# Weight transfers of a recurrent-attention loop issued by SyncE and ScalarE in turn

## The chip, the cores and the metric

The kernel runs on one core of a Trainium2 chip. The metric is device time in microseconds (us). Engines are named as in the profile: PE (TensorE, matmuls), PEld (its weight loads), DVE (VectorE), ACT (ScalarE), POOL (GpSimd), SP (SyncE, which here does nothing but issue transfers). SPq, ACTq and POOLq are the engines' sequencers when they issue DMAs. 16 DMA engines move the data.

## The reference, cut to what matters

Two independent heads, joined along the last axis. Head A is a shifted product and a long convolution over 2048 positions (in the kernel, a transform by matmuls). Head B is a recurrence over 64 segments of 32 rows; the eight memory rows of a segment are the first rows of the output of the one before:

```python
for s in range(n_seg):                      # 64
    h = concatenate([mem, x[:, 32*s:32*s+32]], axis=1)      # 8 + 32 rows, 1024 wide
    q, k, v = (einsum('btd,dhe->bhte', h, W) for W in (Wq, Wk, Wv))   # 32 heads of 128
    p = softmax(where(mask, einsum('bhqe,bhke->bhqk', q, k) * scale, -1e9))
    o = einsum('bhte,hed->btd', einsum('bhqk,bhke->bhqe', p, v), Wo)
    mem = o[:, :8]; outs.append(o[:, 8:])
```

Each segment needs all of Wq, Wk, Wv and Wo, 32 MB in bf16, and no segment can begin before the one before has ended.

## The kernel before, in words

The first 440 us hold head A and everything of head B that doesn't depend on the memory (the projections of the last 8 rows of each segment, written to QKBd and VBd). The rest is the loop of L913: 64 segments, one after another, and it is here that the change lies.

A segment has four groups g of 8 heads. For each group `qk_part` (L740) multiplies by 8 pairs of weight tiles (Wq and Wk, one pair for each 128 rows of the model width), `qk_out` (L752) copies the sums to `qks`, `v_part` (L756) multiplies by 4 pairs of Wv, `tr_a` (L779) transposes q and k, `v_out` (L769) copies v. `scores` (L800), `softmax` (L822) and `pv` (L838) of group g run inside the matmuls of the groups after it; `pv` ends in four copies OT (L853). Then `wo` (L857) multiplies by 4 pairs of Wo for each group into `yacc`. At the turn of the segment ACT copies yacc to Y_sb (L957), PE transposes it (`mt_tp`, L895), DVE puts it into hT (L896), and the next segment's matmuls start from hT. In every fourth segment `wo` also works for 4 x 8 set-aside rows (OTB).

The weights come in 64 pairs of 512 KB. Most of them stay on chip. Two pairs are parked in PSUM and copied into place by ACT and DVE (`unpark`, L711). The other 17, `STREAM` (L42), are read again from DRAM in each segment: qk 2 and 5 of group 0, 3 of group 1, 2 and 6 of groups 2 and 3; v 0 and 3 of group 0, 1 of group 1, 2 of groups 2 and 3; o pair 2 of group 0 (here o0_2), o1_1, o2_0, o2_3 and o3_2. They go through a ring of RING = 4 tiles named `wring` that the parked pairs use too. `place` (L703) takes the next key of the list `todo` (17 x 64 keys in order of use), takes the next ring tile, and issues its transfer; `done` (L720) calls it after the last matmul that reads a pair. So a transfer waits until PE has used the pair that the slot held four places before: o3_2 is put into the slot of o0_2, the next segment's first pair into that of o1_1, and so on.

The kernel is scheduled by hand: each engine does its instructions in the order in which the program writes them. A transfer stands in its issuing engine's queue where `place` is called, and what that engine has behind it waits until it is issued. In the loop SP issues the ring's transfers (L708) and four small loads per segment, qkb (L792). ACT issues one load per segment, H (L657). POOL issues the loads of VB (L797) and the stores (L968, L973).

Of the kernel before, what the change touches and what calls it, by code (L numbers as in the profile page):

```python
# [21 lines left out]
def fused_kernel(ctx: ExitStack, tc, q, k, v, shift_k, ssm_k, ssm_D, outa, x, mem0, Wq, Wk, Wv, Wo, outb, n_seg):  # L22
# [11 lines left out]
    nc = tc.nc  # L34
# [26 lines left out]
    Wst = {key: dram.tile([128, 2, 1024], BF, name=f"Wst{key[0]}{key[1]}_{key[2]}") for key in streamed}  # L61
# [639 lines left out]
    todo = [key for _ in range(n_seg) for key in streamed]  # L701

    def place():  # L703

        if todo:
            key = todo.pop(0)
            t = ring.tile([128, 2, 1024], BF, tag="wring", name="wring")
            nc.sync.dma_start(t[:], Wst[key][:])  # L708
            placed.setdefault(key, []).append(t)

    def unpark():  # L711
# [8 lines left out]
    def done(key):  # L720
        if key in res:
            return
        if key in PARKED:
            t = ring.tile([128, 2, 1024], BF, tag="wring", name="wring")
            placed[PARKED[key]] = [t]
            to_copy.append((PARKED[key], t))
        else:
            place()
# [174 lines left out]
    for _ in range(RING):  # L903
        place()
# [139 lines left out]
```

## Time and profile before

| what | us |
|---|---|
| median of 3 runs | 2319.94 (2311.4 to 2321.02) |
| the profiled execution | 2336.46 |
| its span, first to last instruction | 2334.6 |
| from the first Y_sb (L957) to the last, 63 segments | 1859.8 |
| ring transfers: number, size, median time from issue to landing | 1088, 512 KB, 5.3 to 5.6 |

A page of the profile has the engines' busy time, the span in 40 slices, the DMA queues, the chain of work that ended last (followed back from the last instruction), the costliest groups of instructions and the DMA issues. Further views answer questions on the same execution: the waits (who stood idle for whom), a timeline, and the busy time in stretches that one names. In the lists of queues, q1 is SP's hardware queue, q10 is ACT's, q0 is POOL's.

### The profile page before, as it was taken

The numbers are of one execution on the slowest core, as the hardware profiler recorded it, in microseconds if no ns is written. First come the engines' busy times: TensorE is split into PE (matmuls) and PEld (weight loads), VectorE is DVE, ScalarE is ACT, GpSimd is POOL, SyncE is SP. The second block draws the span as 40 slices with busy tenths as digits, with TensorE's granted clock in tenths as the row PEclk, the third lists the DMA queues.
The fourth block names the chain that finished last, engine by engine and source line by source line (L and its number), as shares of the span: only waits on it lengthen the run. The fifth ranks groups of instructions, "written<-read, shape, count | busy, mean of one in ns | idle before, by whom it ended". The sixth has DMA issues, their size and how long they took to land.

```text
span 2334.6 us, 90400 instructions
## 1 busy us (share of the span) xinstructions
PE 1830.9 (78%) x38867; PEld 1056.3 (45%) x38896; DVE 1023.9 (44%) x3490; ACT 827.8 (35%) x2294; POOL 586.3 (25%) x1177
## 2 busy tenths in 40 slices
PE   5779887588787778787877887888787878888875
PEld 3332233345444445454545454545454545554543
DVE  6878722244433344444444443343444343434442
ACT  5457611233333333333333333333333333333332
POOL 4005612013131213122213131313131313131312
PEclk8999989799999999999999999999999998999998
DMA  7799796899988999999899998999999998989995
GB/s 267 261 342 364 264 357 260 299 329 325 314 296 304 301 313 315 324 314 326 307 318 314 326 316 307 309 339 310 340 307 316 315 334 295 332 302 322 314 326 184
DMA packets 279035, 724.19 MB, mean 310 GB/s; under 512 B 78171, under 2 KB 91435, under 8 KB 278121
## 3 DMA queue, kind: packets, MB, share of 16 engines
q1 hardware_dynamic: 239246, 677.88, 82.9%
q0 software_dynamic: 30496, 34.31, 4.6%
q8 instruction: 304, 4.98, 0.8%
q10 hardware_dynamic: 8892, 6.23, 0.8%
q14 instruction: 97, 0.79, 0.1%
HBM read 672.01 MB, written 55.05 MB: 311 GB/s over the span
## 4 chain that ended last, share of the span: by engine, by line
DMA 48%; PE 30%; issue 5%; DVE 2%; ACT 2%; POOL 1%; SPq 0%; POOLq 0%; ACTq 0%; DVEq 0%
DMA wring<-Wstv 22%; DMA wring<-Wstqk 13%; DMA wring<-Wsto 10%; PE qkacc L748 10%; PE yacc L869 8%; PE vacc L763 4%; PE otacc L848 2%; PE tp L776 1%; PE otacc L850 1%; DMA QKBd<-stq 1%; ACT Y_sb L957 1%; PE S L804 1%; PE mt_tp L895 1%; ACT OT L853 1%; DMA Wo<-in_B_Wo_dram 0%
## 5 line engine op out<-in xcount | busy, mean ns | idle before, releaser
L748 PE MATMUL qkacc<-Wqk,hT 128*32 128x512 bf16 x6144 | 520.9, 400 | 4.8 <-issue 1.1
L855 POOL COPY OTB<-OT 128x64 bf16<-128x64 bf16 x256 | 61.0, 238 | 1363.8 <-ACT OT L853 1363.8
L853 ACT CAST OT<-otacc 128x80 bf16<-128x80 f32 x1024 | 181.5, 230 | 504.3 <-PE otacc L850 497.3
L763 PEld LDWEIGHTS <-hT 128*32 128x32 bf16 x8192 | 227.4, 98 | 247.8 <-issue 165.3
L748 PEld LDWEIGHTS <-hT 128*32 128x32 bf16 x8192 | 184.6, 98 | 303.8 <-issue 169.5
L748 PE MATMUL qkacc<-wring,hT 128*32 128x512 bf16 x2048 | 214.1, 405 | 106.7 <-DMA wring<-Wstqk 104.7
L869 PEld LDWEIGHTS <-OT 128*32 128x32 bf16 x8192 | 224.6, 98 | 125.9 <-issue 112.5
L869 PE MATMUL yacc<-Wo,OT 128*32 128x256 bf16 x5632 | 270.3, 282 | 8.3 <-issue 8.0
L763 PE MATMUL vacc<-wring,hT 128*32 128x256 bf16 x3072 | 146.2, 281 | 144.4 <-DMA wring<-Wstv 143.0
L763 PE MATMUL vacc<-Wv,hT 128*32 128x256 bf16 x5120 | 227.1, 278 | 0.0
L785 DVE COPY QT<-tp 128x256 bf16<-128x256 bf16 x256 | 74.3, 290 | 310.3 <-PE tp L776 309.7
L818 DVE TENSOR_REDUCE mx<-S 128x4 f32<-128x160 f32 x256 | 83.1, 325 | 283.6 <-PE S L815 283.6
L869 PE MATMUL yacc<-wring,OT 128*32 128x256 bf16 x2560 | 145.6, 282 | 73.3 <-DMA wring<-Wsto 67.2
L771 ACT CAST vsb<-vacc 128x256 bf16<-128x256 f32 x256 | 95.3, 372 | 242.0 <-PE vacc L763 240.5
L754 ACT CAST qks<-qkacc 128x512 bf16<-128x512 f32 x256 | 149.5, 584 | 75.4 <-PE qkacc L748 70.3
L714 ACT COPY wring<-park 128x1024 bf16<-128x1024 bf16 x128 | 129.9, 1015 | 107.2 <-PE qkacc L748 101.4
L848 PE MATMUL otacc<-PT,vsb 32*128 32x64 bf16 x2048 | 149.6, 193 | 22.6 <-ACT OT L853 21.5
L797 POOL DMA_DIRECT2D VB<-VBd x256 | 150.9, 596 | 28.2 <-issue 18.5
L824 ACT ACTIVATE E<-S 128x160 bf16<-128x160 f32 x256 | 77.6, 303 | 213.6 <-PE qkacc L748 114.8
L850 PE MATMUL otacc<-PT,VB 32*128 32x64 bf16 x2048 | 145.7, 189 | 3.7 <-issue 3.7
L888 DVE COPY hT<-x_tp 128x192 bf16<-128x192 bf16 (+1 forms) x64 | 16.5, 258 | 294.9 <-PE x_tp L887 294.9
L973 POOL DMA_DIRECT2D out_dram<-YB x256 | 126.7, 502 | 42.2 <-DMA out_dram<-YB 23.5
(213 smaller groups left out, 2900.8 us busy)
## 6 DMA issues: line engine op xcount, KB each, us to landing
wring<-Wstqk SPq DMA_DIRECT2D x448, 512.0 KB, 5.3
wring<-Wstv SPq DMA_DIRECT2D x320, 512.0 KB, 5.4
wring<-Wsto SPq DMA_DIRECT2D x320, 512.0 KB, 5.6
SK<-s_sb SPq DMA_DIRECT2D x8, 1024.0 KB, 6.8
SU<-s_sb SPq DMA_DIRECT2D x8, 1024.0 KB, 6.4
QKBd<-stq POOLq DMA_DIRECT2D x4, 2048.0 KB, 9.9
Kg<-SK SPq DMA_DIRECT2D x16, 512.0 KB, 7.2
Ug<-SU SPq DMA_DIRECT2D x16, 512.0 KB, 8.1
```

The source lines that it names most:

```text
L714: nc.scalar.copy(t[:, 0, :], park[key][0][:])
L748: nc.tensor.matmul(u.qk[p0:p0 + 32, :], lhsT=hT[:, kc, :], rhs=w[:, t, c2 * 512:(c2 + 1) * 512], start=(kc == 0), stop=(kc == 7), tile_pos ...
L754: nc.scalar.copy(u.qks[:], u.qk[:])
L763: nc.tensor.matmul(u.vacc[32 * c:32 * c + 32, 0:256], lhsT=hT[:, kc, :], rhs=w[:, kc % 2, c * 256:(c + 1) * 256], start=(kc == 0), stop=(k ...
L771: nc.scalar.copy(u.v[:], u.vacc[:, 0:256])
L797: nc.gpsimd.dma_start(VB[32 * c:32 * c + 32, :], VBd[8 * s:8 * s + 8].rearrange("r (g c x) -> c g r x", g=4, c=4)[c])
L818: nc.vector.tensor_reduce(out=mx[:], in_=S[:], op=ALU.max, axis=AX.X)
L848: nc.tensor.matmul(o, lhsT=u.v[r, i * 128:(i + 1) * 128], rhs=PTv[r, i, 0], start=True, stop=False, tile_position=(32 * c, 0))
L850: nc.tensor.matmul(o, lhsT=VB[r, i * 128:(i + 1) * 128], rhs=PTv[r, i, 1], start=False, stop=True, tile_position=(32 * c, 0))
L853: nc.scalar.copy(u.OT[:, 2 * c:2 * c + 2, :], ov[:, :, 0:40])
L869: nc.tensor.matmul(Y[32 * dq:32 * dq + 32, 256 * n:256 * n + 256], lhsT=lhsT, rhs=w[:, hh % 2, dq * 256:(dq + 1) * 256], start=(u.g == 0 a ...
L973: nc.gpsimd.dma_start(outb[r0:r0 + 8, dq * 256:(dq + 1) * 256], YB[32 * dq + 8 * jj:32 * dq + 8 * jj + 8, :])
```

## The change

One line of `place`. The transfer was always issued by SP; now it is issued by SP when the number of keys left is odd, and by ACT when it is even.

```diff
             key = todo.pop(0)
             t = ring.tile([128, 2, 1024], BF, tag="wring", name="wring")
-            nc.sync.dma_start(t[:], Wst[key][:])
+            (nc.sync if len(todo) % 2 else nc.scalar).dma_start(t[:], Wst[key][:])
             placed.setdefault(key, []).append(t)
```

The matmuls, the ring, the keys and their order are the same. In the program that is built, 544 of the 1088 transfers stand in ACT's queue among its copies and activations. As each segment has 17 of them, what SP issues in one segment ACT issues in the next.

## The prediction

> **What bounds the kernel now.** I read the page first (shares, slices, chain), then the waits of PE, then stretches of one segment of the loop (L913), then SyncE's issues, and last the one place where two hardware queues already run together.
>
> ```profile
> PE 1830.9 (78%) x38867; PEld 1056.3 (45%) x38896; DVE 1023.9 (44%) x3490; ACT 827.8 (35%) x2294; POOL 586.3 (25%) x1177
> ...
> q1 hardware_dynamic: 239246, 677.88, 82.9%
> ...
> DMA 48%; PE 30%; issue 5%; DVE 2%; ACT 2%; POOL 1%; SPq 0%; POOLq 0%; ACTq 0%; DVEq 0%
> ```
>
> The chain that ended last is half DMA. ACT is busy a third of the time, so it has room; SyncE's and ACT's issuing is 0% of the chain. The issuing is therefore not the bottleneck.
>
> ```profile
> PE vacc L763 <- DMA wring<-Wstv: 143.0, 187, 3.0
> ...
> PE yacc L869 <- DMA wring<-Wsto: 67.2, 108, 2.7
> PE otacc L848 <- ACT OT L853: 21.5, 63, 0.3
> ```
>
> These are PE's waits inside the loop (total us, times, longest). With 81.9 us on Wstqk, PE stands still 292 us for streamed weights over 64 segments, 4.6 us in each. ACT holds it 0.34 us once per segment.
>
> ```profile
> 1518.00:1526.00 8.00, 5.44 (x130) 3.21 (x122) 2.14 (x9) 1.38 (x6) 3.62 (x8) 0.88 0.96 327
> 1526.00:1528.00 2.00, 2.00 (x32) 0.82 (x28) 0.78 (x2) 0.92 (x1) 1.10 (x3) 0.65 0.79 281
> 1528.00:1530.00 2.00, 2.00 (x52) 1.26 (x48) 0.24 (x2) 1.23 (x4) 0.00 (x0) 1.00 0.64 189
> 1530.00:1546.00 16.00, 14.11 (x392) 8.94 (x384) 9.21 (x38) 6.43 (x23) 0.71 (x3) 1.00 1.00 368
> ```
>
> Columns: stretch, us, busy us of PE, PEld, DVE, ACT, POOL, then PEclk, DMA share, GB/s. The first row is the end of a segment and its turn (the mean segment is 29.5 us, from the starts of Y_sb L957). DMA is full for 16 us, nearly full at the end, and idles only after the turn: then all four ring slots hold data that PE has not reached. So the loop is a closed circle: a slot is consumed, refilled, and lands 5.3 to 5.6 us later (part 6 of the page), and the 16 engines are the bound except at the turn. More bandwidth is to be had only there.
>
> **The turn, where the change bites.**
>
> ```profile
> 1517.85 0.32 SPq L708 DMA_DIRECT2D wring<-Wsto  x1
> 1518.50 1.47 SPq L708 DMA_DIRECT2D wring<-Wstqk  x2
> ...
> 1523.61 0.40 PE L869 MATMUL yacc<-wring,OT 128*32 128x256 bf16 x8 [1.48 <-DMA wring<-Wsto]
> ...
> 1524.37 0.37 ACT L957 CAST Y_sb<-yacc 128x256 bf16<-128x256 f32 x1 [2.53 <-PE yacc L869]
> ```
>
> The last transfer of the segment (o, group 3, pair 2) is issued at 1517.85 and PE waits 1.48 us for it, until 1523.61. Everything behind it hangs on it: yacc, Y_sb, the transpose, hT and the next segment's first matmul. The two transfers issued behind it (1518.50 and 1519.5) are wanted only after the turn: PE reads the first at 1526.38. One queue serves them in order, so they do not disturb it.
>
> **What the change does, part by part.** L708 issues 1088 transfers. By the parity of the remaining list 544 stay on SyncE and 544 go to ACT. Neighbours always go to different queues; 17 per segment is odd, so two segments take opposite halves. Bytes, ring and consumption stay; PE, DVE and POOL keep their order.
>
> *Sharing between the queues* is the largest term. At the start of the kernel L259 loads KS_nat from both queues; the DMA view of 5 to 10 us shows
>
> ```profile
> DMA packets 567, 2.06 MB, mean 413 GB/s; under 512 B 63, under 2 KB 63, under 8 KB 567
> ...
> q1 hardware_dynamic: 283, 1.03, 51.2%
> q10 hardware_dynamic: 284, 1.04, 51.0%
> ```
>
> Packets of the same 4 KB rows pass turn by turn, half each, and the engines are full either way; the loop's full stretch is at share 1.00 from one queue. So two queues give no bandwidth, they only change the order: a transfer at the head of one queue runs at half rate while the other queue has work. At 413 GB/s 524,288 bytes take 1.27 us. If o3_2 starts together with its neighbour on the other queue, it lands 1.27 us later; if they are half a transfer apart, 0.64 us; if the neighbour is late, 0. PE then waits so much longer, and the DMA idles so much longer after the turn. I take 0.64, in the middle: the issues from 1517.85 to 1520.77 come 0.65 to 1.25 us apart, around one service time. 63 turns x 0.64 = 40 us (0 to 80). Inside the full 16 us an older transfer also lands later, but the next one no later than before, and a full DMA loses nothing; I set that at 0, and upwards 20 us (63 x 0.3).
>
> By the Trainium skill (DMA: Bandwidth & Descriptors, section "Queues, rings and completion order") each DMA engine goes round its queue rows packet by packet; 283 against 284 packets agree.
>
> *ACT's time.* A SyncE issue takes 0.32 us (L708 above). ACT's own: KS_nat (the same 4 KB rows) 0.39 to 0.86, median 0.45; H (L657, short rows) 0.55. I take 0.45: 544 x 0.45 = 245 us on an engine that is idle 1507 us. An ACT issue waits for PE to finish the slot's old weights, and all that stands behind it in ACT's order needs a later PE step, so the wait itself holds nothing up. What counts is the issue's length, at two places. (a) Behind o3_2 the refill stands ahead of Y_sb: released at 1524.0 it ends at 1524.5, Y_sb began at 1524.37, so 0.14 us later in the half of segments where this refill is ACT's: 32 x 0.14 = 4.5 us. (b) Behind o2_3 it stands ahead of the four copies L853 that PE waits for: SyncE issued at 1520.77, ACT would end at 1521.22, the copies began at 1521.03: 32 x 0.19 = 6 us. At 0.32 these are 0 and 2, at 0.86 18 and 19. Together 10 (2 to 37). The copies qks and vsb behind other issues have over 1 us of matmuls (v_part) or a whole group in hand; if that cover went, each 0.45 us would come on top (third rival).
>
> *SyncE's time* is a gain. 97 of its L708 issues come 0.04 us behind another issue with no wait of their own, often behind a qkb load (L792, 0.43 us). Half of them move, each at most 0.43 us earlier, 0.2 in the mean: 48 x 0.2 = 10 us, of which PE feels what it was waiting for. I take 5 (0 to 22; the upper end: SyncE issues for 1088 x 0.32 + 256 x 0.43 = 458 us, 24% of the loop's 1880, so a release meets a running issue with that chance and waits half of it, 0.04 us per transfer, 44 us, of which half moves).
>
> The four small queues (VB, stores, H) now share with two big queues instead of one. VB lands 4.8 us after issue and is wanted a third of a segment later, H a group later: nothing.
>
> Sum: 40 + 10 - 5 = +45 us. On the profiled execution's own 2336.5 us (span 2334.6) that gives 2381; that execution lay 16.5 us above the median 2319.9, which I carry over: **2365 us**.
>
> **Rivals.**
>
> *Only the issue time moves, no change* (0.18). If the transfers settle half a period apart, completions keep their rhythm and the last one is late by little; then +10 - 5 remains: 2325. For it: DMA is full at share 1.00 in the long stretch. Against: PE waits for precisely the last transfer. The Trainium skill says so on the same page, section "Issuing engines are not separate DMA queues": several issuers save only the sequencer's time. By that rule the result would lie here.
>
> *Faster* (0.21). SyncE's serial issuing is the mechanism: a slot that comes free while SyncE issues a qkb load or an earlier refill waits, and the circle turns later. If all 22 us of that lateness were PE's, and sharing and ACT cost nothing, 2298. It decides where a refill that was late is the one PE stands for (the 187 waits of L763). Against: 0% SPq in the chain, and most issues come right behind a PE step.
>
> *Much slower* (0.14). Each ACT issue delays a copy that PE or PSUM is waiting for: a third of 245 us on top of the 45, 2447; or full sharing, 80 + 37: 2437. For it: S, tp and otacc banks are few. Against: PE's waits for ACT are 35 us now.
>
> *The change does nothing* can be left out: ACT's order in the changed program has the 544 transfers.
>
> **How the numbers follow.** My forecast, slower by 12 to 90 us, has 0.47. With the much slower case that is 0.61 slower, 0.18 within, 0.21 faster (0.5% is 11.6 us, about what a measurement tells from no change). The range takes in the bounds of sharing and ACT (2320 + 0 + 2 to 2320 + 80 + 37, 2322 to 2437), cut where the tails hold less than 1 in 10 each, and half of the faster case: 2298 to 2415.
>
> **What would show it.** L708 appears as 544 on SPq and 544 on ACTq, queue q10 carries about 290 MB. PE yacc <- DMA Wsto grows from 67 us to about 105; the Wsto landing from 5.6 to over 6 us; DMA share in the loop falls a little. PE otacc <- ACT OT grows from 21 by under 10 us. I am wrong if Wsto waits do not grow (no sharing, or sharing hidden), if waits for ACT grow by tens of us, or if the waits on Wstv fall by 20 us or more (SyncE was holding them).

## The result, and the profile after

The changed kernel takes 2464.6 us in the median of four runs (2444.5 to 2481.3), the kernel before 2320.5 beside it. The profiled execution is the slowest of the four (2481.3 us, span 2479.4) and had the lowest granted clock (0.909, the others 0.913 to 0.922); the ratio leaves it out as a slow run. That ratio is 1.059, 95% interval 1.049 to 1.069: the kernel is slower, as forecast, but by some 137 us and not by 45.

The page of the changed kernel, in the same order as that of before:

```profile
PE 1885.9 (76%) x38896; PEld 1078.6 (44%) x38896; DVE 1024.4 (41%) x3490; ACT 833.8 (34%) x2294; POOL 586.2 (24%) x1177
...
q1 hardware_dynamic: 160910, 392.63, 46.0%
q10 hardware_dynamic: 87228, 291.47, 33.8%
...
DMA 46%; PE 33%; issue 5%; ACT 2%; POOL 1%; DVE 1%; ACTq 1%; SPq 0%; POOLq 0%; DVEq 0%
...
L748 PE MATMUL qkacc<-Wqk,hT 128*32 128x512 bf16 x6144 | 552.3, 423 | 2.3 <-DVE hT L888 0.4
```

The same line L748 on the page of before:

```profile
L748 PE MATMUL qkacc<-Wqk,hT 128*32 128x512 bf16 x6144 | 520.9, 400 | 4.8 <-issue 1.1
```

q10, ACT's queue, now carries 291 MB, so the change does what it says. ACT is as busy as before. In the profiled executions PE is busy 55 us longer with the same matmuls; the 6144 of L748 take 423 ns each instead of 400. PE's waits in the loop of the changed kernel (total us, times, longest):

```profile
PE vacc L763 <- DMA wring<-Wstv: 174.8, 131, 5.1
PE yacc L869 <- DMA wring<-Wsto: 113.7, 104, 5.0
PE qkacc L748 <- DMA wring<-Wstqk: 95.3, 96, 3.6
PE otacc L848 <- ACT OT L853: 26.0, 63, 0.5
```

The line on Wstqk in the kernel before:

```profile
PE qkacc L748 <- DMA wring<-Wstqk: 81.9, 103, 2.1
```

The waits for streamed weights grew from 292 to 384 us: 47 on Wsto, 32 on Wstv, 13 on Wstqk. They are not more numerous but longer (Wstv 131 instead of 187, the longest 5.1 us instead of 3.0). With 55 us of PE's own time and 5 on OT that is 152 us, against 145 us of span between the two profiled executions.

Counted by pair in the two traces, from the second segment on, the growth lies mainly in two of the seventeen streamed pairs. PE waits 94 us for v1_1 where it waited 32, and 60 us for o3_2 where it waited 20; the other fifteen rose and fell, in sum from 240 to 227 us. PE waits as long for v1_1 in the segments where SP issues it (48 us in 32 segments) as where ACT does (46 us in 31), so the queue of ACT is not the slower one.

The middle of the loop, 600 to 2200 us, before and then after (busy us of PE, PEld, DVE, ACT, POOL; PEclk, DMA share, GB/s at the end):

```profile
600.00:2200.00 1600.00, 1280.56 (x31532) 780.94 (x31528) 647.59 (x2590) 536.93 (x1688) 393.52 (x859) 0.95 0.91 315
```

```profile
600.00:2200.00 1600.00, 1234.26 (x29500) 746.53 (x29496) 606.79 (x2427) 506.53 (x1580) 363.97 (x797) 0.91 0.87 295
```

The DMA engines, which were nearly full, stand idle more, and the clock is lower. One place where it is seen, from the timeline of the changed kernel:

```profile
1503.45 1.35 SPq L708 DMA_DIRECT2D wring<-Wstqk  x2
...
1504.20 0.33 ACTq L708 DMA_DIRECT2D wring<-Wstv  x1
...
1510.84 0.40 PE L763 MATMUL vacc<-wring,hT 128*32 128x256 bf16 x8 [2.30 <-DMA wring<-Wstv]
```

SP issues qk1_3 at 1503.45 and qk2_2 at 1504.48; between them, at 1504.20, ACT issues v1_1. PE needs them in the order qk1_3, v1_1, qk2_2, and stands 2.30 us for v1_1, which takes 6.6 us. An ACT issue lasts 0.33 us.

### The profile page after: what moved, and what is told of

Read it like the earlier page. It is cut to its first block, busy times and chain, and to the rows that moved or that the text cites. A ratio compares the mean times of both kernels' runs of the same rounds, so it can differ in the third digit from the quotient of the medians.

```text
span 2479.4 us, 90275 instructions
## 1 busy us (share of the span) xinstructions
PE 1885.9 (76%) x38896; PEld 1078.6 (44%) x38896; DVE 1024.4 (41%) x3490; ACT 833.8 (34%) x2294; POOL 586.2 (24%) x1177
## 4 chain that ended last, share of the span: by engine, by line
DMA 46%; PE 33%; issue 5%; ACT 2%; POOL 1%; DVE 1%; ACTq 1%; SPq 0%; POOLq 0%; DVEq 0%
DMA wring<-Wstv 23%; PE qkacc L748 13%; DMA wring<-Wsto 12%; DMA wring<-Wstqk 9%; PE yacc L869 8%; PE vacc L763 5%; PE otacc L848 2%; PE tp L776 2%; PE otacc L850 1%; DMA QKBd<-stq 1%; ACT Y_sb L957 1%; PE S L804 1%; PE mt_tp L895 1%; PE idle L880 1%; ACTq L708 0%
## 5 line engine op out<-in xcount | busy, mean ns | idle before, releaser
L748 PE MATMUL qkacc<-Wqk,hT 128*32 128x512 bf16 x6144 | 552.3, 423 | 2.3 <-DVE hT L888 0.4
L763 PEld LDWEIGHTS <-hT 128*32 128x32 bf16 x8192 | 231.7, 100 | 271.2 <-issue 214.0
L748 PEld LDWEIGHTS <-hT 128*32 128x32 bf16 x8192 | 190.5, 102 | 336.5 <-issue 212.7
L748 PE MATMUL qkacc<-wring,hT 128*32 128x512 bf16 x2048 | 226.8, 430 | 119.7 <-DMA wring<-Wstqk 118.4
L869 PE MATMUL yacc<-Wo,OT 128*32 128x256 bf16 x5632 | 275.7, 288 | 10.4 <-issue 10.1
L968 POOL DMA_DIRECT2D out_dram<-Y_sb x256 | 131.3, 523 | 38.8 <-ACT Y_sb L957 30.0
```

The source lines that it names most:

```text
L748: nc.tensor.matmul(u.qk[p0:p0 + 32, :], lhsT=hT[:, kc, :], rhs=w[:, t, c2 * 512:(c2 + 1) * 512], start=(kc == 0), stop=(kc == 7), tile_pos ...
L763: nc.tensor.matmul(u.vacc[32 * c:32 * c + 32, 0:256], lhsT=hT[:, kc, :], rhs=w[:, kc % 2, c * 256:(c + 1) * 256], start=(kc == 0), stop=(k ...
L869: nc.tensor.matmul(Y[32 * dq:32 * dq + 32, 256 * n:256 * n + 256], lhsT=lhsT, rhs=w[:, hh % 2, dq * 256:(dq + 1) * 256], start=(u.g == 0 a ...
L968: nc.gpsimd.dma_start(outb[32 * s:32 * s + 24, dq * 256:(dq + 1) * 256], Y_sb[32 * dq + 8:32 * dq + 32, :])
```

## The experiments

The theory after the result: the two queues share the engines, the transfer that PE needs next lands late, and this costs inside the segment as well as at the turn; PE's clock falls in the longer waits and adds to it. The rivals: ACT's time, the number of queues or issues as such, and SyncE's issuing. All medians stand beside runs of the kernel before on the same chip; each edit is to the kernel before unless it says otherwise. Edits of several lines move the line numbers a little.

**All on ACT.**

```diff
-            nc.sync.dma_start(t[:], Wst[key][:])
+            nc.scalar.dma_start(t[:], Wst[key][:])
```

> All 1088 ring transfers go out from ACT, in one queue and in order; ACT issues twice as many as in the changed kernel. Order theory (the loss comes from two queues sharing the DMA engines, so that the transfer PE waits for lands late): 2320 to 2350 us, since the order is kept and ACT's issues cost 10 to 30 us; PE's waits on Wsto near 67 us. Rival, ACT's time (the issues hold up ACT's copies): 2465 us or more, up to 2610, twice the loss of the changed kernel.

2349.1 us against 2327.5, ratio 1.011 (1.008 to 1.014). With twice the issues on ACT most of the loss is gone. The waits of PE:

```profile
PE yacc L869 <- DMA wring<-Wsto: 53.8, 92, 2.1
PE otacc L848 <- ACT OT L853: 36.5, 66, 1.1
PE mt_tp L895 <- ACT Y_sb L957: 30.0, 63, 1.0
```

The waits on Wsto are even shorter than before; those on ACT's copies OT and Y_sb are 32 us longer (before 21.5 and 13.0). So 1088 issues on ACT cost some 26 us, at the two places that the prediction named, and 544 should cost about half of that. In the changed kernel itself the wait for OT grew by 4.5 us and that for Y_sb not at all. ACT's time is a small part of the loss and not its cause.

**Each transfer cut into rows, one half from each queue, and the control.**

```diff
-            nc.sync.dma_start(t[:], Wst[key][:])
+            nc.sync.dma_start(t[0:64], Wst[key][0:64])
+            nc.scalar.dma_start(t[64:128], Wst[key][64:128])
```

> Each transfer is cut in two, rows 0 to 63 from SP and 64 to 127 from ACT: both queues are used all the time, by halves of the same pair, so the order of the pairs is kept. Order theory: 2310 to 2350 us. Rival, two queues (they make the packets or the issuing slower by themselves): 2440 us or more. Rival, ACT's time: 2465 us or more, as ACT issues 1088 times.

2941.5 us, ratio 1.265 (1.260 to 1.270): far outside what the order theory allowed. But the packets of 4 KB took 272 ns in the median where they took 159, so the cut itself was suspect. The control issues both halves from SP (`nc.sync` in both lines):

> The cut into rows 0 to 63 and 64 to 127 of the second experiment, both halves from SP: it tells whether the 26% there came from two queues or from the shape of the cut. If from the shape (64 rows of one transfer are spread over all 16 engines): over 2800 us and packets of 4 KB that take some 270 ns again. If from two queues: 2320 to 2400 us and packets near 160 ns.

3030.3 us, 1.303 (1.297 to 1.309). The shape costs it, with one queue too; with two queues it is even a little less. This pair says nothing about the change, except that a tile must not be halved by partitions here.

**Cut into columns, one half from each queue, and the control.**

```diff
-            nc.sync.dma_start(t[:], Wst[key][:])
+            nc.sync.dma_start(t[:, 0, :], Wst[key][:, 0, :])
+            nc.scalar.dma_start(t[:, 1, :], Wst[key][:, 1, :])
```

> Each transfer is cut along the columns: the Wq (or first) half of every pair from SP, the second half from ACT, all 128 partitions in each. Both queues are at work at once, but on the same pair, so the order of the pairs is kept. The packets are 2 KB; the next run has the same cut from SP alone. Order theory: within 40 us of that run (ACT issues 1088 times, which cost 27 us when it issued whole transfers). Rival, two queues slow the transfers by themselves whatever their order: over 100 us above that run.

> The same cut along the columns, both halves from SP: what the smaller packets and 2176 issues of SP cost without a second queue. Both theories: 2320 to 2420 us; a 2 KB packet took 84 ns where a 4 KB packet took 159, 5% on a DMA that is full for most of the segment, so up to 100 us.

2409.1 us with two queues (1.039, 1.033 to 1.045) and 2455.0 with SP alone (1.058, 1.053 to 1.062). When both queues always work on the same pair, two queues are 46 us faster than one. PE's waits for the copies OT are 85 us with two queues (1088 ACT issues) and 22 with one, yet its waits for weights are 239 against 329. The expectation had allowed a difference of 40 us, and part of the 46 may be the 2176 issues that SP alone has to make. So a second queue does no harm by itself; which pairs the two carry does. Why the cut costs SP alone 131 us, more than the packets' 5%, stays open.

**One queue around the turn, two inside the segment.**

```diff
-            nc.sync.dma_start(t[:], Wst[key][:])
+            pos = (len(streamed) * n_seg - 1 - len(todo)) % len(streamed)
+            on_act = 4 <= pos < 15 and len(todo) % 2 == 0
+            (nc.scalar if on_act else nc.sync).dma_start(t[:], Wst[key][:])
```

> The transfers around the turn (o2_3, o3_2 and the next segment's first four) all stay on SP; the eleven between them alternate, 352 from ACT. Order theory, with its weight at the turn: 2350 to 2400 us; PE's waits on Wsto back near 67 us and the clock back near 0.94. If the order inside the segment matters as much: 2400 to 2440. Rival, ACT's time: 352/544 of the loss, about 2415 us, with the Wsto waits as they were.

**A queue for each segment, in turn**, so that the queues meet only at the turn.

```diff
-            nc.sync.dma_start(t[:], Wst[key][:])
+            seg = (len(streamed) * n_seg - 1 - len(todo)) // len(streamed)
+            (nc.scalar if seg % 2 else nc.sync).dma_start(t[:], Wst[key][:])
```

> All 17 transfers of one segment go out from SP, all of the next from ACT: 544 from ACT as in the changed kernel, but two queues are at work together only at the turn, where the next segment's first transfers share with the last of this one. Order theory: 2390 to 2440 us, PE's waits on Wsto over 100 us and a lower clock at the turn, its waits on Wstv near 143 us as before. Rival, ACT's time: 2465 us.

Around the turn in one queue: 2394.9 us, 1.030 (1.025 to 1.034). The queue changed by segment: 2366.4 us, 1.020 (1.015 to 1.025), less than expected. Their waits, first the one with the turn on SP:

```profile
PE vacc L765 <- DMA wring<-Wstv: 199.0, 171, 4.2
...
PE yacc L871 <- DMA wring<-Wsto: 62.4, 94, 2.1
```

and the one with a queue for each segment:

```profile
PE vacc L764 <- DMA wring<-Wstv: 123.4, 169, 3.2
PE yacc L870 <- DMA wring<-Wsto: 88.7, 116, 3.1
```

Each lengthens the waits that it was meant to: inside the segment Wstv (143 before, 199 now) with Wsto as before, at the turn Wsto (67 before, 89 now) with Wstv not longer. Counted by pair, the first has its growth at v1_1 (87 us of waiting, 32 before) and the second at o3_2 (39, before 20). In time 67 us come from inside and 39 from the turn, ACT's issues included (by the first experiment 8 and 13 us). The sharing costs more inside, where the prediction had put nothing. The two make 106 us of the 137; what the rest is was not separated.

**SyncE relieved of the qkb loads.**

```diff
-        nc.sync.dma_start(u.qkb[:], QKBd[g][:, s, :])
+        nc.scalar.dma_start(u.qkb[:], QKBd[g][:, s, :])
```

> The kernel before with the 256 small qkb loads (L792) issued by ACT; all ring transfers stay on SP. It tests the rival of the prediction that SyncE's serial issuing holds transfers up. That rival: 2295 to 2310 us. Order theory: 2315 to 2335 us, no gain, since SP's issuing was not on the path.

2322.6 us against 2324.0, ratio 1.001 (0.998 to 1.004). The qkb issues on SyncE held nothing up. Whether a refill that stands behind another refill in SyncE's queue is held up was not taken apart.

**Only v1_1 on ACT.** In the profile of the changed kernel the longest waits came about 11 us into the segment, for v1_1.

```diff
-            nc.sync.dma_start(t[:], Wst[key][:])
+            pos = (len(streamed) * n_seg - 1 - len(todo)) % len(streamed)
+            (nc.scalar if pos == 5 else nc.sync).dma_start(t[:], Wst[key][:])
```

> Only one of the 17 transfers of a segment, v1_1, goes to ACT; the sixteen others stay on SP. Order theory: PE's longest wait of the changed kernel is for v1_1, about 11 us into the segment, and it comes from the shared engines, not from the number of issues: 2335 to 2375 us, waits on Wstv grow from 143 to 165 us or more. Rival, the loss goes with the number of ACT's issues: 64 of 544, 12% of 137 us or 16 us at most, and by the experiment with all transfers on ACT 2 us; waits on Wstv as before.

2380.8 us against 2322.6, ratio 1.023 (1.018 to 1.027): 64 transfers out of 1088 cost 58 us by the medians and 52 by the ratio, a little more than was expected. From its timeline, in one segment:

```profile
1602.24 4.37 SPq L709 DMA_DIRECT2D wring<-Wstqk  x3
...
1603.42 0.32 ACTq L709 DMA_DIRECT2D wring<-Wstv  x1
...
1609.41 0.40 PE L764 MATMUL vacc<-wring,hT 128*32 128x256 bf16 x8 [1.91 <-DMA wring<-Wstv]
```

SP issues qk1_3 at 1602.24, ACT v1_1 at 1603.42, SP qk2_2 at 1603.68, a quarter of a microsecond after it. The DMA view of 1606.5 to 1607.5 and of 1607.5 to 1608.5, while PE waits for v1_1 (q10):

```profile
q1 hardware_dynamic: 56, 0.22, 62.1%
q10 hardware_dynamic: 39, 0.15, 39.2%
```

```profile
q1 hardware_dynamic: 63, 0.24, 69.3%
q10 hardware_dynamic: 34, 0.13, 32.5%
```

In these two microseconds the younger qk2_2 in q1 gets some two thirds of the engines' time, and v1_1, the only transfer in its queue, one third. In the kernel before qk2_2 stood behind v1_1. Over all segments v1_1 lands 6.5 us after its issue in the median (where the trace has the landing), against 5.3 in the kernel before:

```profile
wring<-Wstv ACTq DMA_DIRECT2D x64, 512.0 KB, 6.5
```

The late transfer holds up a refill too. qk3_2 goes into the slot of v1_1, four places on in the ring, so it can't be issued before PE has read v1_1. It went out 0.94 us behind the transfer ahead of it in the kernel before, and 2.25 us behind it here (medians; 2.21 in the changed kernel).

**v1_1 and qk2_2 on ACT.** If that is the cause, it goes when the younger one is put behind the older again, though ACT then issues twice as many (the edit is shown against the run just above):

```diff
-            (nc.scalar if pos == 5 else nc.sync).dma_start(t[:], Wst[key][:])
+            (nc.scalar if pos in (5, 6) else nc.sync).dma_start(t[:], Wst[key][:])
```

> As the run before with v1_1 on ACT, but its younger neighbour qk2_2 goes to ACT too, behind it in the same queue: 128 transfers from ACT instead of 64. If v1_1 is late because the younger qk2_2 overtakes it from the other queue: 2318 to 2345 us, and the waits on Wstv fall from 196 back to 130 to 160 us. If a transfer from ACT's queue is late by itself, or if ACT's issues cost: 2380 us or more, Wstv waits over 190 us.

2332.4 us against 2326.9, ratio 1.003 (1.001 to 1.006). The waits on Wstv, first with v1_1 alone on ACT, then with both:

```profile
PE vacc L764 <- DMA wring<-Wstv: 196.3, 196, 3.8
```

```profile
PE vacc L764 <- DMA wring<-Wstv: 156.0, 202, 3.0
```

The landing of v1_1 is back at 5.4 us after its issue, and qk3_2 goes out 1.26 us behind the transfer ahead of it:

```profile
wring<-Wstv ACTq DMA_DIRECT2D x64, 512.0 KB, 5.4
```

One more transfer on ACT in each segment and nearly the whole loss is gone. This separates the theory from its rivals: ACT's time, the number of ACT's issues, and a slower ACT queue would each have made it worse.

**PE kept at work in the waits of the changed kernel.** `add_zero` multiplies a tile of zeros (`zero`) by resident weights and adds the result to the sums, which stay what they are.

```diff
+    def add_zero(acc, n):
+        for _ in range(n):
+            for c in range(4):
+                nc.tensor.matmul(acc[32 * c:32 * c + 32, 0:256], lhsT=zero[:], rhs=res[("qk", 0, 0)][:, 0, 0:256],
+                                 start=False, stop=False, tile_position=(0, 32 * c))
...
+            if u.g == 1 and kc == 2:          # v_part, ahead of v1_1
+                add_zero(u.vacc, 8)
...
+            if u.g == 3 and hh == 4:          # wo, ahead of o3_2
+                add_zero(Y, 8)
```

> The changed kernel with matmuls that add zero (8 x 4 of them, some 0.9 us at full clock) ahead of the reading of o3_2 into yacc and ahead of v1_1 into vacc, the two places where PE now waits longest; the output is the same. If part of the loss is PE's clock that falls in the longer waits (PE busy time grew by 55 us for the same matmuls): 2400 to 2440 us and a granted clock over 0.93. If the clock is only a companion of the waits: 2465 us or more, up to 2520.

2430.9 us, ratio to the kernel before 1.045 (1.038 to 1.053), where the changed kernel has 1.059: some 32 us less, with 4096 matmuls more. The line that had grown to 423 ns:

```profile
L748 PE MATMUL qkacc<-Wqk,hT 128*32 128x512 bf16 x6144 | 510.6, 393 | 4.5 <-DVE hT L899 0.4
```

The granted clock of its runs is 0.951 to 0.953, that of the changed kernel's 0.909 to 0.922. So part of the loss, about 32 of the 137 us, is the clock that falls in the longer waits. The intervals of the two ratios overlap a little, so the size is rough.

**The same in the kernel before**, 4 x 4 matmuls ahead of o3_2 alone.

> The kernel before with 4 x 4 matmuls that add zero (some 0.4 us at full clock) ahead of the reading of o3_2, the same output. If PE's clock at the turn (0.88 in the mean there) is what the waits cost on top: 2290 to 2312 us. If the added matmuls delay PE as often as they fill a wait: 2320 to 2345 us.

2337.0 us against 2322.6, ratio 1.004 (1.001 to 1.007). The clock rose from 0.954 to 0.959 in the mean of the runs, and the time did not fall: the added matmuls delay PE at least as much as they gain. No version was found that beats the kernel before.

## Why the prediction was right and wrong

*The direction and the mechanism* were right: two queues bring no bandwidth, they change the order, and the transfer that PE waits for lands late. Wrong was that this would cost nothing inside the segment.

*Sharing at the turn*, forecast at 40 us, held. Waits on Wsto grew by 47 us in the changed kernel, 40 of them at o3_2, and the kernel in which the queues meet only at the turn lost 39 us, some 13 of them ACT's issues. The 0.64 us for each turn was only the middle of 0 to 1.27, so that it fits this well is partly luck.

*Sharing inside the segment*, set at 0 and upwards 20 us, is the step that failed. The prediction said that "a full DMA loses nothing", because the next transfer lands no later than before. What it left out is that PE takes the pairs in order: while it waits for the older one, the younger one is of no use to it, the slot of the older one isn't given back, and the next refill goes out later (qk3_2 by 1.3 us). In the changed kernel Wstv and Wstqk took 45 us more in sum and v1_1 alone 62 more, in the kernel with one queue around the turn 67 us were lost, and a single transfer overtaken in each segment cost 58 us, nearly all of which came back when the overtaking was taken away. Why it is v1_1 that is hit was not tested; in the kernel before, its younger neighbour is issued 0.49 us behind it in the median, the shortest distance of any two, which is the likely reason. In the changed kernel the DMA is no longer full (share 0.87 for 0.91); with v1_1 alone on ACT the share stays at 0.91 and only the rate falls, from 315 to 308 GB/s. So a share of 1.00 over 16 us was no reserve against a lost order.

*PE's clock* was in no term. The prediction showed rows with PEclk 0.88 and 0.65 around the turn and didn't ask what longer waits would do to them. PE's busy time grew by 55 us in the profiled execution; about 32 us of the loss went when PE was kept at work.

*ACT's time*, forecast at 10 us (2 to 37), was small as said: 26 us for twice the issues, and 4.5 us of longer OT waits in the changed kernel. An issue took 0.33 us, not the 0.45 that was assumed. *SyncE's gain*, 5 us, did not show: 1.001 with the qkb loads taken away. The count of 97 issues 0.04 us behind another, on which that term stood, isn't in the trace, where 2 come that close and 155 within 0.2 us.

*The rivals.* "Faster" had SyncE's issuing as its mechanism; the qkb experiment excludes it for the qkb loads, and the waits on Wstv rose where it needed them to fall. "No change" had the completions keeping their rhythm; the overtaking shows that they don't. "Much slower" gave about the time that came out (2437 to 2447), but through ACT's copies or through more sharing at the turn, and neither was it.

*The signs named in advance.* 544 issues on each queue, 291 MB on q10, Wsto waits of 114 for about 105, a lower DMA share and an OT wait grown by under 10 us came as written. The Wsto landing did not rise over 6 us; the recorded landings, half of all, are 5.4 (SP) and 5.3 (ACT). Neither did any of the three signs of being wrong come: none of them would have shown that the waits on Wstv grow.

The rule that the prediction cited from the Trainium skill (DMA: Bandwidth & Descriptors, "Issuing engines are not separate DMA queues"), that several issuers save only issue time, agrees with the runs as far as bandwidth goes: the two queues moved no more than one (295 GB/s for 315). Here no saving was seen, and the change cost 5.9%.

## What to carry to other kernels

Here one queue kept the transfers in the order of need. If consumption is in order and the slots are few, then splitting the stream over two queues can let a younger transfer overtake the one that is waited for, and the wait holds up the refills behind it, however full the DMA looks. If two queues must be used, put neighbours that are issued close together in the same one, and look at PE's clock when its waits grow.

## What the runs showed of the hardware

Two queues need not move equal shares. At the start of the kernel they had 283 and 284 packets in 5 us, but in the two windows of the v1_1 experiment 56 to 39 and 63 to 34. The trace doesn't tell which of the 16 engines moved a packet, so it stays open whether single engines shared unevenly or some had nothing left of v1_1 to move.

A 512 KB transfer cut at partition 64 into two of 256 KB made 4 KB packets take 279 ns with one queue and 272 with two (600 to 2200 us) instead of 159, with the DMA share at 1.00 and 230 GB/s on one queue where the uncut one had 0.91 and 315: 30% of the kernel's time. Cut along the columns the same bytes cost 5.8%.
